# Feed-forward products in pairs of 64x128 tiles: a recurrent attention layer followed by a squared-ReLU feed-forward

## The chip, the cores and the metric

One NeuronCore of a Trainium2 chip runs the whole program. The metric is the device time of one execution in microseconds (us); lower is better. The engines are PE (TensorE: matrix products and transposes, with weight loads of their own), DVE (VectorE), ACT (ScalarE), POOL (GpSimd) and SP (SyncE, which here only issues DMAs).

## The reference

Four batches of eight heads, 768 steps, head dimension 40. Each head has a 40x40 state that is read, decayed and updated at every step; the outputs of all heads, put side by side, are the 320 features of 3072 tokens, which pass through a feed-forward of 320 to 2048 to 320 with a squared ReLU between.

```python
for t in range(S):                                # S = 768, state is B x H x D x D
    y[:, :, t] = einsum('bhd,bhde->bhe', rt, state)
    Sa = einsum('bhde,bhe->bhd', state, at)
    state_decay = state * wt[:, :, None, :] - einsum('bhd,bhe->bhde', Sa, bt)
    state = state_decay + einsum('bhd,bhe->bhde', vt, kt)
x = y.transpose(0, 2, 1, 3).reshape(B * S, H * D)  # 3072 x 320
h = x @ w_in                                       # 320 x 2048
g = maximum(h, 0) ** 2
out = g @ w_out                                    # 2048 x 320
```

## The kernel before

The steps are worked in 12 chunks of 64 steps, all 32 heads at once, so that a chunk gives 256 tokens. `load(c)` issues the six inputs of a chunk on SP, two DMAs each, into buffers that two chunks share in turn. `prep(c)` takes the logarithm of w on ACT, splits it in two bf16 parts (`hi`, `lo`), forms running sums and their exponentials on PE and ACT (`ci`, `cf`, `ei`, `ex`, `ef`), scales k and b (`mulKB`), casts a, r and v, and transposes them on PE (`TK`, `TA`, `TR`); `EN` is the first triangular product. `rec(c)` solves for the updates (`AS`, `EV`, `NU`) and carries the state on (`SC`, `S`, `TS`). `read(c)` has the outputs (`TV`, `CX`, `RS`, `Y`), multiplies them with the decay (`y`, and `yd` for 64 columns once more behind the 320), and transposes the 320 features of the 256 tokens (`XT`, copied by `xt`) into the tile `XT`, 3 x 256 columns on 128 partitions: two tiles of 128 features, and a third that holds the last 64 features on both partition halves.

`ffn(c)` is the feed-forward of the chunk's 256 tokens. The 2048 hidden units are four groups `u` of 512.

- `F c u`: 8 full products, weights of 128 features x 128 units from `WIN`, 256 columns.
- `FL c u`: the last 64 features, 4 products with weights of 64 x 128 from `WLAST`; the two halves of PE's rows take two products at a time (shape "R"). `FL` stands behind `F` for even `u` and before it for odd `u`.
- `f c u` applies the ReLU from PSUM into `G` (ACT or DVE), `q c u` squares it (DVE, POOL or ACT).
- `O c u`: 8 products with weights of 128 units x 128 tokens from `G` against 320 columns of `WOUT`; two halves `g` of the tokens lie in the two PSUM banks of one buffer. `o c` copies both halves, 128 x 640, to `osb`, `st c` stores them.

Every PE operation has a shape, the second argument of `pe`: "D" is the full 128 x 128 array, "R" two tiles of 64 rows, "C" two of 64 columns, "Q" 64 x 64 tiles. PSUM is used as four buffers `pb0` to `pb3` of two banks; the number behind PE in the order says which one an operation takes.

The program has no scheduler of its own. `ORDER` is a text of 1,030 or so entries, "engine operation", written out for all 12 chunks, and `Plan.issue` emits the operations in that order; each engine then runs its own operations in that order and waits by semaphore where data or buffers are not ready. The weights of the feed-forward are loaded in the first part of SP's queue (`lwl`, `lwi`, `lwo`) into the buffers of `G` and `osb`, and cast from there (`cwl`, `cwi`, `cwo`).

```python
ORDER = """SP ldw 0; SP lda 0; SP ldb 0; SP ldk 0; ACT ln 0; SP ldw 1; POOL hi 0; ...
... PE F 10 u3; ACT q 10 u1; PE0 F 11 u0; ACT f 10 u3; PE2 F 11 u2; ACT q 10 u0; DVE q 10 u3;
PE FL 11 u0; PE1 FL 11 u3; PE FL 11 u2; PE3 FL 11 u1; ACT f 11 u0; PE F 11 u1; ...
```

Of the kernel before, what the change touches and what calls it, by code (L numbers as in the profile page):

```python
# [84 lines left out]
HALVES = ()  # L85
O_AFTER = 0
ORDER = """SP ldw 0; SP lda 0; SP ldb 0; SP ldk 0; ACT ln 0; SP ldw 1; POOL hi 0; POOL castA 0; DVE lo 0; PE0
TA 0; SP lda 1; PE1 ci 0 h0; PE2 ci 0 h1; ACT ex 0 h0 g1; PE3 cf 0; ACT ex 0 h1 g0; ACT ei 0 h1;
ACT ex 0 h1 g1; ACT ei 0 h0; SP ldv 0; ACT ef 0; DVE mulKB 0 h1; SP ldw 2; ACT ex 0 h0 g0; DVE
mulKB 0 h0; DVE tA 0 g0; PE2 TK 0; DVE tK 0; ACT ln 1; SP ldk 1; POOL hi 1; DVE tA 0 g1; PE3 EN 0  # L90
g0; POOL lo 1; DVE mEN 0 g0; PE1 EN 0 g1; DVE mEN 0 g1; SP ldb 1; PE2 ci 1 h1; POOL castV 0 g0;
ACT ei 1 h1; POOL castV 0 g1; ACT ex 1 h1 g1; ACT ex 1 h1 g0; POOL castA 1; PE0 EV 0; SP ldr 1;
PE3 cf 1; ACT u0 0; PE1 ci 1 h0; ACT ln 2; PE NU 0; ACT ex 1 h0 g1; PE2 TA 1; POOL hi 2; ACT ef 1;
SP lda 2; DVE lo 2; ACT u1 0 g0; DVE tA 1 g0; ACT ei 1 h0; SP ldv 1; PE3 S 0 g0; DVE tA 1 g1; ACT
ex 1 h0 g0; ACT u1 0 g1; PE1 ci 2 h0; SP ldr 0; ACT ex 2 h0 g1; PE S 0 g1; DVE mulKB 1 h0; PE2 TV
0; DVE mulKB 1 h1; ACT ei 2 h0; DVE s 0 q1; ACT tV 0; SP ldw 3; PE0 TK 1; DVE s 0 q0; SP ldk 2;
DVE tK 1; PE3 TS 0; ACT tS 0; PE2 EN 1 g1; PE0 cf 2; DVE mEN 1 g1; SP ldb 2; PE3 EN 1 g0; ACT ef
2; POOL castR 0; DVE mEN 1 g0; ACT ex 2 h0 g0; POOL castV 1 g1; ACT castA 2; PE2 TR 0; PE0 ci 2
h1; POOL castV 1 g0; ACT tR 0 g0; PE1 AS 1; SP lwl 0; ACT tR 0 g1; POOL castR 1; PE EV 1; ACT ln
3; PE3 CX 0 g0; PE2 CX 0 g1; ACT u0 1; POOL hi 3; DVE mCX 0 g0; ACT ex 2 h1 g1; PE NU 1; POOL lo  # L100
3; ACT ex 2 h1 g0; SP lwi 0 u0; ACT ei 2 h1; DVE mCX 0 g1; PE3 TR 1; ACT u1 1 g0; PE0 TA 2; ACT tR
1 g1; DVE tA 2 g1; PE2 Y 0; SP ldv 2; ACT tR 1 g0; ACT u1 1 g1; PE3 SC 1; DVE mulKB 2 h1; PE1 TV
1; SP ldr 2; PE S 1 g0; DVE tA 2 g0; ACT tV 1; PE S 1 g1; DVE y 0; DVE mulKB 2 h0; ACT cwl 0; DVE
yd 0; PE0 TK 2; DVE s 1 q0; PE1 ci 3 h1; POOL cwi 0 u0; SP lwi 0 u1; PE2 CX 1 g0; DVE tK 2; ACT ei
3 h1; ACT ex 3 h1 g0; ACT ex 3 h1 g1; SP lwo 0 x1; DVE s 1 q1; PE0 cf 3; PE1 EN 2 g0; DVE mCX 1
g0; ACT ef 3; PE3 TS 1; POOL castV 2 g1; SP lwo 0 x0; ACT tS 1; DVE mEN 2 g0; PE0 EN 2 g1; POOL
castR 2; PE2 AS 2; SP ldb 3; POOL castV 2 g0; DVE mEN 2 g1; PE3 ci 3 h0; PE1 XT 0; ACT ex 3 h0 g0;
POOL cwi 0 u1; ACT ei 3 h0; DVE xt 0; PE EV 2; ACT ex 3 h0 g1; SP lwi 0 u3; PE0 CX 1 g1; ACT u0 2;
PE1 FL 0 u1; DVE mCX 1 g1; PE NU 2; SP lda 3; PE3 RS 1; ACT u1 2 g0; PE0 SC 2; PE Y 1; DVE u1 2
g1; SP ldk 3; PE F 0 u1; DVE y 1; SP lwi 0 u2; DVE yd 1; PE S 2 g0; ACT f 0 u1; PE S 2 g1; PE2 TR  # L110
2; DVE s 2 q0; PE3 FL 0 u3; ACT tR 2 g1; POOL cwi 0 u3; DVE s 2 q1; ACT tR 2 g0; SP ldw 4; DVE q 0
u1; POOL castA 3; PE F 0 u3; POOL cwo 0 x0; PE1 TV 2; ACT f 0 u3; DVE cwo 0 x1; PE2 XT 1; PE0 TS
2; SP lwo 0 x2; ACT tV 2; PE3 F 0 u0; DVE tS 2; POOL mulKB 3 h0; DVE xt 1; PE0 TA 3; PE FL 0 u0;
SP lwo 0 x3; DVE tA 3 g1; PE2 FL 1 u3; ACT f 0 u0; PE1 CX 2 g0; POOL cwi 0 u2; DVE tA 3 g0; PE F 1
u3; SP ldv 3; DVE mulKB 3 h1; PE3 F 1 u2; ACT f 1 u3; DVE mCX 2 g0; SP ldr 3; PE0 TK 3; ACT ln 4;
PE FL 1 u2; PE2 FL 1 u1; DVE tK 3; PE1 CX 2 g1; ACT f 1 u2; POOL hi 4; PE F 1 u1; POOL cwo 0 x2;
DVE mCX 2 g1; PE3 F 1 u0; POOL lo 4; ACT cwo 0 x3; PE0 EN 3 g0; ACT f 1 u1; SP lwo 0 x5; PE FL 1
u0; DVE mEN 3 g0; PE1 F 0 u2; ACT f 1 u0; SP lwo 0 x4; PE FL 0 u2; DVE q 0 u0; PE2 EN 3 g1; POOL
castV 3 g0; PE0 cf 4; ACT f 0 u2; DVE mEN 3 g1; PE3 ci 4 h0; SP ldw 5; POOL castV 3 g1; ACT ef 4;
PE1 RS 2; DVE q 0 u2; PE Y 2; ACT ei 4 h0; PE2 AS 3; DVE yd 2; PE EV 3; DVE cwo 0 x5; ACT ex 4 h0  # L120
g1; DVE y 2; PE0 O 0 u0; SP lwo 0 x7; ACT u0 3; POOL cwo 0 x4; DVE q 1 u0; ACT ex 4 h0 g0; POOL
castR 3; ACT q 0 u3; PE1 ci 4 h1; SP lwo 0 x6; PE NU 3; ACT ex 4 h1 g1; PE3 TR 3; ACT u1 3 g0; SP
ldk 4; PE O 0 u1; DVE tR 3 g1; ACT ex 4 h1 g0; DVE u1 3 g1; ACT ei 4 h1; PE O 0 u2; POOL cwo 0 x7;
SP ldb 4; ACT tR 3 g0; ACT ln 5; PE1 XT 2; DVE cwo 0 x6; PE2 TV 3; SP lda 4; POOL hi 5; DVE xt 2;
PE3 SC 3; ACT tV 3; PE S 3 g0; POOL lo 5; PE S 3 g1; PE O 0 u3; DVE s 3 q1; SP ldv 4; DVE s 3 q0;
POOL q 1 u1; PE1 ci 5 h0; ACT o 0; PE2 CX 3 g0; SP ldk 5; PE3 cf 5; ACT ex 5 h0 g0; DVE mCX 3 g0;
PE0 FL 2 u1; ACT ef 5; PE F 2 u1; DVE mulKB 4 h0; ACT ex 5 h0 g1; PE2 F 2 u2; ACT f 2 u1; SP ldb
5; DVE mulKB 4 h1; POOL castA 4; PE3 FL 2 u3; PE FL 2 u2; ACT ei 5 h0; DVE q 2 u1; PE0 TK 4; ACT f
2 u2; PE1 TA 4; PE F 2 u3; DVE tA 4 g0; SP ldw 6; DVE tK 4; PE2 F 2 u0; POOL castV 4 g0; ACT f 2
u3; POOL castV 4 g1; PE FL 2 u0; DVE tA 4 g1; PE0 ci 5 h1; POOL q 2 u3; ACT f 2 u0; PE3 CX 3 g1;  # L130
PE1 O 1 u0; SP lda 5; DVE mCX 3 g1; ACT ex 5 h1 g1; ACT q 2 u0; PE2 EN 4 g1; PE3 EN 4 g0; POOL q 1
u2; DVE mEN 4 g1; PE O 1 u1; ACT ex 5 h1 g0; ACT ei 5 h1; SP st 0; DVE mEN 4 g0; PE0 RS 3; PE Y 3;
POOL mulKB 5 h0; SP ldr 4; PE2 AS 4; DVE y 3; PE EV 4; DVE q 1 u3; PE O 1 u2; SP ldw 7; DVE yd 3;
ACT ln 6; DVE mulKB 5 h1; PE O 1 u3; ACT u0 4; POOL hi 6; POOL q 2 u2; PE NU 4; ACT o 1; PE3 XT 3;
ACT u1 4 g0; PE0 TS 3; SP st 1; DVE xt 3; PE1 TK 5; ACT tS 3; DVE u1 4 g1; PE3 FL 3 u3; POOL castA
5; PE F 3 u3; SP ldv 5; DVE tK 5; POOL castR 4; PE2 TA 5; ACT f 3 u3; POOL lo 6; PE0 TV 4; SP lda
6; DVE tA 5 g1; PE1 O 2 u0; DVE tA 5 g0; DVE tV 4; ACT ln 7; PE3 SC 4; PE S 4 g0; SP ldb 6; PE S 4
g1; PE2 ci 6 h0; DVE s 4 q0; PE0 TR 4; ACT ex 6 h0 g0; PE O 2 u1; SP ldk 6; ACT ei 6 h0; DVE s 4
q1; ACT ex 6 h0 g1; DVE tR 4 g1; ACT tR 4 g0; PE3 cf 6; PE2 EN 5 g0; ACT ef 6; POOL castV 5 g1; PE
O 2 u2; DVE mEN 5 g0; SP ldr 5; POOL castV 5 g0; ACT q 3 u3; PE0 CX 4 g0; PE3 ci 6 h1; DVE mCX 4  # L140
g0; PE2 CX 4 g1; ACT ei 6 h1; POOL hi 7; PE O 2 u3; ACT castA 6; POOL lo 7; DVE mCX 4 g1; PE0 F 3
u0; ACT ex 6 h1 g0; ACT o 2; ACT ex 6 h1 g1; PE FL 3 u0; SP st 2; PE2 EN 5 g1; PE1 TA 6; ACT f 3
u0; DVE mEN 5 g1; PE3 RS 4; PE Y 4; SP ldw 8; ACT q 3 u0; PE0 AS 5; POOL mulKB 6 h1; DVE yd 4; PE
EV 5; DVE tA 6 g1; PE2 FL 3 u1; DVE y 4; SP ldv 7; ACT u0 5; PE F 3 u1; POOL mulKB 6 h0; DVE tA 6
g0; PE3 F 3 u2; SP ldv 6; ACT f 3 u1; PE FL 3 u2; POOL castR 5; PE1 XT 4; PE2 TK 6; ACT f 3 u2;
DVE xt 4; POOL q 3 u1; PE NU 5; DVE tK 6; SP ldr 6; PE1 TR 5; ACT u1 5 g0; PE3 F 4 u0; DVE tR 5
g1; ACT tR 5 g0; ACT u1 5 g1; PE FL 4 u0; PE2 EN 6 g1; PE1 EN 6 g0; ACT f 4 u0; DVE mEN 6 g1; PE0
SC 5; SP lda 7; PE S 5 g0; PE S 5 g1; ACT q 3 u2; PE3 ci 7 h0; DVE s 5 q1; PE2 O 3 u0; SP ldk 7;
ACT ei 7 h0; DVE mEN 6 g0; ACT ex 7 h0 g1; PE O 3 u1; ACT ex 7 h0 g0; SP st0 0; DVE s 5 q0; POOL
castV 6 g0; PE3 TV 5; PE1 ci 7 h1; DVE tV 5; POOL castR 6; PE0 TS 4; ACT ex 7 h1 g1; SP ldb 7; PE  # L150
O 3 u2; ACT ei 7 h1; POOL castA 7; DVE tS 4; ACT ex 7 h1 g0; ACT ln 8; SP ldr 7; PE3 CX 5 g0; PE1
# [808 lines left out]
```

## Time and profile before

| | |
|---|---|
| median of 3 runs | 252.59 us (251.22, 252.59, 256.84) |
| span of the profiled execution | 249.1 us, mean granted PE clock 0.985 |
| device time of the profiled execution | not listed by itself; the runs lie 2.1, 3.5 and 7.7 us above its span |
| busy: PE, weight loads, DVE, ACT, POOL | 219.2, 171.4, 183.3, 172.4, 119.3 us |
| products on PE | 5752 |
| first and last group of products begin | 8.1 us, 239.4 us (`O 11 u0`) |
| `WOUT` products, 128 x 320 | 384, 57.2 us in all |
| `WIN` products, 128 x 256 | 384, 48.4 us |
| `WLAST` products, 64 x 256 | 192, 17.4 us |
| DMA | 33.58 MB, 135 GB/s over the span |

The span is the time from the first to the last instruction; the device time of a run has the start and the end around it. Busy time of PE is a union: products overlap in the pipeline, and the mean duration of one (some 0.27 us) is longer than the distance between two starts. A duration of a group is therefore no price of one product; the distance of starts is.

### The profile page before, as it was taken

The numbers are of one execution on the slowest core, as the hardware profiler recorded it, in microseconds if no ns is written. First come the engines' busy times: TensorE is split into PE (matmuls) and PEld (weight loads), VectorE is DVE, ScalarE is ACT, GpSimd is POOL, SyncE is SP. The second block draws the span as 40 slices with busy tenths as digits, with TensorE's granted clock in tenths as the row PEclk, the third lists the DMA queues.
The fourth block names the chain that finished last, engine by engine and source line by source line (L and its number), as shares of the span: only waits on it lengthen the run. The fifth ranks groups of instructions, "written<-read, shape, count | busy, mean of one in ns | idle before, by whom it ended". The sixth has DMA issues, their size and how long they took to land.

```text
span 249.1 us, 12580 instructions
## 1 busy us (share of the span) xinstructions
PE 219.2 (88%) x5752; PEld 171.4 (69%) x5752; DVE 183.3 (74%) x227; ACT 172.4 (69%) x231; POOL 119.3 (48%) x119
## 2 busy tenths in 40 slices
PE   0458868859997999999999999999999999999991
PEld 0336856647775777787778878877777787877770
DVE  7585869786976889976877958788778889746121
ACT  2548898737995876688759788896798351863930
POOL 4261332416746598383488881534369930452000
PEclk9999997799999999999999999999999999999999
DMA  6999899989998986978868978965580020201121
GB/s 130 168 157 212 158 190 182 229 195 218 224 195 161 157 199 122 189 159 147 184 171 136 179 121 217 157 163 115 119 144 4 4 58 4 56 3 30 26 52 55
DMA packets 115179, 33.58 MB, mean 135 GB/s; under 512 B 101302, under 2 KB 115126, under 8 KB 115126
## 3 DMA queue, kind: packets, MB, share of 16 engines
q1 hardware_dynamic: 114982, 32.62, 65.3%
q8 instruction: 45, 0.74, 1.2%
q10 hardware_dynamic: 144, 0.16, 0.2%
q14 instruction: 8, 0.07, 0.1%
HBM read 28.84 MB, written 3.93 MB: 132 GB/s over the span
## 4 chain that ended last, share of the span: by engine, by line
PE 51%; SPq 21%; DMA 8%; DVE 6%; ACT 6%; issue 4%; POOL 3%; POOLq 0%; ACTq 0%
PE pb L384 45%; SPq L407 8%; PE pb L388 5%; SPq L431 3%; SPq L421 3%; SPq L400 2%; SPq L882 2%; SPq L414 2%; DMA osb<-in_moe_w_out_dram 2%; DMA G<-in_moe_w_in_dram 2%; DMA raw_w<-in_w_dram 2%; DMA raw_r<-in_r_dram 2%; DVE AR L365 1%; ACT AR L370 1%; DMA out_dram<-osb 1%
## 5 line engine op out<-in xcount | busy, mean ns | idle before, releaser
L384 PE MATMUL pb<-WOUT,G 128*128 128x320 bf16 x384 | 57.2, 300 | 1.1 <-DVE WOUT L365 1.1
L802 ACT ACTIVATE G<-pb 128x1024 bf16<-128x1024 f32 x44 | 44.6, 1021 | 19.3 <-PE pb L384 18.4
L810 POOL TENSOR_TENSOR G<-G 128x1024 bf16<-128x1024 bf16 x21 | 40.8, 1956 | 24.2 <-ACT G L802 24.1
L384 PE MATMUL pb<-XT,WIN 128*128 128x256 bf16 x384 | 48.4, 273 | 2.8 <-POOL WIN L374 2.8
L384 PEld LDWEIGHTS <-G 128*128 128x128 bf16 x384 | 35.3, 98 | 15.8 <-issue 2.3
L384 PEld LDWEIGHTS <-WIN 128*128 128x128 bf16 x384 | 34.9, 98 | 10.4 <-POOL WIN L374 3.3
L578 DVE TENSOR_TENSOR CX<-pb,MSKI 128x1024 bf16<-128x1024 f32 x24 | 29.0, 1220 | 7.4 <-PE pb L384 7.3
L578 DVE TENSOR_TENSOR EN<-pb,MSK 128x1024 bf16<-128x1024 f32 x24 | 29.0, 1221 | 6.5 <-PE pb L384 6.2
L481 ACT ACTIVATE Gin<-pb 64x320 f32<-64x320 f32 x48 | 20.6, 429 | 9.8 <-PE pb L384 9.2
L374 POOL CAST VU<-raw_v 64x640 bf16<-64x640 f32 x24 | 18.7, 777 | 11.8 <-DMA raw_v<-in_v_dram 11.1
L370 ACT ACTIVATE osb<-pb 128x640 f32<-128x640 f32 (+1 forms) x13 | 8.3, 640 | 18.6 <-PE pb L384 18.1
L670 DVE TENSOR_TENSOR STb<-pb,GT 64x640 bf16<-64x640 f32 x22 | 18.0, 820 | 2.9 <-PE pb L384 2.6
L374 POOL CAST hi<-lnW 128x640 bf16<-128x640 f32 x12 | 9.0, 747 | 22.7 <-ACT lnW L453 19.4
L380 DVE TENSOR_TENSOR KB<-raw_kb,iG 128x640 bf16<-128x640 f32 x16 | 15.6, 992 | 5.7 <-DMA raw_kb<-in_b_dram 3.2
L384 PEld LDWEIGHTS <-EN 64*64 64x64 bf16 x768 | 15.3, 114 | 5.9 <-issue 2.7
L475 ACT ACTIVATE iG<-pb 128x640 f32<-128x640 f32 x24 | 16.7, 696 | 3.4 <-PE pb L384 3.2
L553 DVE TENSOR_TENSOR AR<-pb,GT 128x512 bf16<-128x512 bf16 x24 | 15.8, 683 | 2.3 <-PE pb L388 2.0
L384 PE MATMUL pb<-XT,WLAST 64*128 64x256 bf16 x192 | 17.4, 274 | 0.1
L808 DVE TENSOR_TENSOR G<-G 128x1024 bf16<-128x1024 bf16 x13 | 10.4, 805 | 8.6 <-ACT G L802 8.5
L370 ACT ACTIVATE VUT<-pb 128x2048 bf16<-128x2048 bf16 x8 | 15.0, 1874 | 2.2 <-PE pb L388 2.2
L370 ACT ACTIVATE VU<-pb 64x640 bf16<-64x640 f32 x19 | 13.2, 696 | 3.7 <-PE pb L384 3.5
L378 POOL TENSOR_TENSOR KB<-raw_kb,iG 128x640 bf16<-128x640 f32 x8 | 12.6, 1584 | 6.2 <-ACT iG L475 4.5
(82 smaller groups left out, 417.5 us busy)
## 6 DMA issues: line engine op xcount, KB each, us to landing
raw_w<-in_w_dram SPq DMA_DIRECT2D x24, 160.0 KB, 4.5
raw_a<-in_a_dram SPq DMA_DIRECT2D x24, 160.0 KB, 4.4
raw_kb<-in_b_dram SPq DMA_DIRECT2D x24, 160.0 KB, 4.3
...
```

What stands on the lines that cost most here:

```text
L370: alts.append(("ACT", c_act(n), lambda: nc.scalar.activation(out=o_(), in_=i_(), func=ACTF.Copy, scale=1.0 if scale is None else scale)))
L374: lambda: nc.gpsimd.tensor_copy(out=o_(), in_=i_())))
L380: ("DVE", c_dve(n), lambda: nc.vector.tensor_tensor(out=o_(), in0=a_(), in1=b_(), op=op))]
L384: return lambda: nc.tensor.matmul(out=o_(), lhsT=l_(), rhs=r_(), start=start, stop=stop, skip_group_check=True)
L407: nc.sync.dma_start(out=raw_kb[c % NKBR][rows(g if nm == "b" else 1 - g), NJ * g:NJ * g + NJ, :], in_=half(x, g))
L475: ew(f"ei {c} h{jh}", [("ACT", c_act(2 * n), lambda hb=hb, jh=jh: nc.scalar.activation(out=iG[0][:].rearrange("p (g j) e -> p g (j e)", g= ...
L481: nc.scalar.activation(out=Gin[c % NGI][rows(g), NP * jh:NP * jh + NP, :].rearrange("p j e -> p (j e)"), in_=slot(hb, FP32)[rows(g), g, 0: ...
L553: ew(f"tA {c} g{g}", [("DVE", c_dve(512), lambda g=g: nc.vector.tensor_tensor(out=steps(AR[q2][:, 0, g]), in0=turned(ha, g), in1=steps(GT[ ...
L578: evac(f"m{nm} {c} g{g}", lambda s, n: [("DVE", c_dve(n), lambda: nc.vector.tensor_tensor(out=dst[q2][:, g, s].rearrange("p q i t -> p (q ...
L670: ew(f"s {c} q{q}", [("DVE", c_dve(2 * n), lambda q=q: nc.vector.tensor_tensor(out=STb[q2][rows(q), :, q, 0:D], in0=slot(hs, FP32)[rows(q) ...
L802: ("ACT", c_act(1024), lambda gb=gb, hf=hf: nc.scalar.activation(out=gb, in_=slot(hf, FP32)[:], func=ACTF.Relu)),
L810: ("POOL", 1900, lambda gv=gv: nc.gpsimd.tensor_tensor(out=gv, in0=gv, in1=gv, op=ALU.mult)),
```

## The change

The tile `XT` becomes five tiles of 256 columns. Partitions 0 to 63 of tile k hold features 64k to 64k+63, partitions 64 to 127 the next 64, which for the last tile are the first 64 again (`yd` now copies columns 0 to 64). `XT` on PE has 20 transposes for 12, and `xt` copies 1280 columns for 768. `F` has 20 products with weights of 64 x 128, in ten pairs: the two partition halves work on two different blocks of units and two different tiles of features. `FL` is gone. `O` is split by `g`; for each, 32 products with 64 units each run in 16 pairs, one partition half into each PSUM bank of a buffer, so that the two banks have to be added: `oa` copies the first bank on ACT to `osb`, `o` adds the second on DVE. The last chunk's `O` keeps full products, in one bank for each `g`. The pieces of w_in are loaded by partition halves, 64 x 4 x 256 instead of 128 x 2 x 256. Constants and helpers that are not used any more are taken out (`evac` and `both` split nothing before). `ORDER` is written anew for all engines.

```diff
-    XT = buf("XT", [128, 3, NT], BF16, 2)
+    XT = buf("XT", [128, 5, NT], BF16, 2)
...
-    WIN = buf("WIN", [128, 2, DFF], BF16)[0]
+    WIN = buf("WIN", [128, 4, 4, 256], BF16)[0]
...
-        ew(f"yd {c}", out_y(n - 64, n, n), reads=[hy] + GIN, writes=[("Yb", q2, 1)],
+        ew(f"yd {c}", out_y(0, 64, n), reads=[hy] + GIN, writes=[("Yb", q2, 1)],
...
-        for k3 in range(3):
+        for k in range(5):
             for bb in range(2):
                 for g in range(2):
                     ms.append(tp(
...
-                        lambda k3=k3, bb=bb, g=g: Yb[q2][
-                            rows(g), bb, 128 * k3:128 * k3 + 128], g))
+                        lambda k=k, bb=bb, g=g: Yb[q2][
+                            rows(g), bb, 64 * k:64 * k + 128], g))
...
-            lambda: slot(hx, BF16)[:, :, 0:384].rearrange("p g (k t) -> p g k t", t=128),
-            768, True),
+            lambda: slot(hx, BF16)[:, :, 0:640].rearrange("p g (k t) -> p g k t", t=128),
+            1280, True),
...
-            for x in (1, 0) if tail else (0, 1):
-                if x:
-                    pe(f"FL {c} u{u}", "R", NT, ml, **last)
-                else:
-                    pe(f"F {c} u{u}", "D", NT, ms, **wide)
+            for i in range(2):
+                for k in range(5):
+                    for rg in range(2):
+                        f = (k + rg) % 5
+                        ms.append(mm(
+                            lambda rg=rg, i=i, hf=hf: slot(hf, FP32)[:, rg, NT * i:NT * i + NT],
+                            lambda rg=rg, f=f, i=i, u=u: (
+                                WLAST[rows(rg), u] if f == 4 else WIN[rows(rg), u, f])[
+                                :, 128 * i:128 * i + 128],
+                            lambda rg=rg, k=k: XT[q2][rows(rg), k, :],
+                            i == 0 and k == 0, k == 4))
+            pe(f"F {c} u{u}", "R", NT, ms, reads=[("XT", q2), ("WIN", u), ("WLAST",)],
+               writes=[hf], alloc=[hf])
...
+                    for h in range(2):
+                        ms.append(mm(
+                            lambda h=h, ho=ho: slot(ho, FP32)[:, h, 0:DM],
+                            lambda g=g, j=j, h=h: G[q2][
+                                rows(h), j, 2 * g * L:2 * g * L + 2 * L],
+                            lambda j=j, h=h: WOUT[rows(h), j, :], j == 0, j == NFB - 1))
+                pe(f"O {c} g{g}u{u}", "D" if final else "R", DM, ms,
+                   reads=[("G", q2, u), ("WOUT", 2 * u), ("WOUT", 2 * u + 1)],
+                   writes=[ho], alloc=[ho] if u == 0 else [])
+            if not final:
+                ew(f"oa {c} g{g}", copy_alts(
+                    lambda g=g: osb[q2][:, g, :],
+                    lambda ho=ho: slot(ho, FP32)[:, 0, 0:DM], DM, engines=("ACT",)),
+                   reads=[ho], writes=[("osb", q2, g)], free=[ho])
+                ew(f"o {c} g{g}", [("DVE", c_dve(DM), lambda g=g, ho=ho: nc.vector.tensor_tensor(
+                    out=osb[q2][:, g, :], in0=slot(ho, FP32)[:, 1, 0:DM],
+                    in1=osb[q2][:, g, :], op=ALU.add))],
+                   reads=[ho, ("osb", q2, g)], writes=[("osb", q2, g)], free=[ho])
+                continue
```

In the new order the end of the list reads:

```diff
+xt 11; ACT oa 10 g1; PE3 F 11 u2; DVE o 10 g1; ACT f 11 u2; PE0 F 11 u0; POOL q 11 u2; DVE f 11 u0;
+DVE q 11 u0; PE1 F 11 u1; ACT f 11 u1; PE3 F 11 u3; ACT q 11 u1; PE0 O 11 g1u0; SP st 9; DVE f 11
...
```

More of the change, by code (lines that the diff above doesn't have):

```diff
@@ L82, in issue @@
         assert len(done) == len(self.ops)
[L85 to L151, printed above, removed]
@@ new lines @@
+cwi 0 u3; ACT ef 4; SP ldv 3; PE0 ci 4 h0; DVE mulKB 3 h1; ACT ei 4 h0; ACT ex 4 h0 g1; SP ldr 3;
+PE1 F 1 u0; DVE tA 3 g0; DVE tA 3 g1; ACT ex 4 h0 g0; PE3 CX 2 g0; DVE mCX 2 g0; PE2 F 1 u1; PE3 TK
+3; ACT tK 3; DVE f 1 u1; POOL q 0 u1; PE0 RS 2; PE Y 2; POOL cwi 0 u2; POOL cwo 0 x3; DVE y 2; ACT
+f 1 u0; DVE yd 2; PE2 F 0 u3; DVE cwo 0 x2; PE3 EN 3 g1; PE0 F 1 u2; DVE f 0 u3; DVE mEN 3 g1; POOL
+castV 3 g1; ACT f 1 u2; PE1 F 0 u2; SP lwo 0 x5; PE2 EN 3 g0; DVE mEN 3 g0; ACT f 0 u2; PE0 F 1 u3;
@@ new lines @@
+1 u0; POOL cwo 0 x6; POOL mulKB 4 h1; DVE s 3 q1; ACT q 0 u3; DVE s 3 q0; PE0 F 2 u2; ACT f 2 u1;
+DVE hi 5; PE3 TV 3; ACT q 1 u1; PE O 0 g1u3; SP ldw 6; DVE lo 5; ACT f 2 u2; PE O 0 g0u3; SP ldv 4;
+ACT oa 0 g0; DVE tV 3; DVE q 1 u2; PE0 cf 5; POOL castA 4; DVE o 0 g0; PE3 F 2 u3; ACT oa 0 g1; DVE
+o 0 g1; ACT ef 5; POOL castV 4 g0; PE2 F 2 u0; DVE mulKB 4 h0; ACT f 2 u3; PE0 CX 3 g0; PE3 ci 5
+h0; SP ldk 5; ACT f 2 u0; ACT ei 5 h0; PE1 O 1 g0u0; SP ldb 5; DVE mCX 3 g0; PE O 1 g0u1; PE2 TK 4;
@@ new lines @@
+mulKB 5 h0; ACT u1 4 g1; ACT oa 1 g1; POOL mulKB 5 h1; DVE tS 3; PE3 TV 4; DVE o 1 g1; PE1 TK 5;
+PE0 SC 4; ACT f 3 u3; PE S 4 g0; DVE q 2 u3; SP ldv 5; ACT tV 4; DVE tK 5; PE S 4 g1; POOL castA 5;
+DVE s 4 q0; PE2 O 2 g0u0; PE1 ci 6 h0; PE O 2 g0u1; PE3 TA 5; DVE s 4 q1; ACT ex 6 h0 g1; PE O 2
+g0u2; POOL castR 4; PE O 2 g0u3; SP ldr 5; ACT ex 6 h0 g0; SP ldb 6; DVE tA 5 g0; ACT ei 6 h0; DVE
+tA 5 g1; PE1 EN 5 g0; PE0 TR 4; ACT oa 2 g0; DVE o 2 g0; POOL castV 5 g1; ACT tR 4 g1; PE3 O 2
+g1u0; DVE mEN 5 g0; ACT tR 4 g0; PE O 2 g1u1; PE2 CX 4 g1; PE0 cf 6; DVE mCX 4 g1; PE O 2 g1u2; PE1
@@ new lines @@
+ACT tK 9; DVE s 8 q1; PE0 ci 10 h0; DVE mCX 8 g1; PE O 6 g0u2; PE O 6 g0u3; PE3 O 6 g1u0; ACT ex 10
+h0 g1; PE1 EN 9 g1; PE O 6 g1u1; ACT oa 6 g0; DVE o 6 g0; ACT ex 10 h0 g0; PE2 CX 8 g0; POOL castV
+9 g1; ACT ei 10 h0; PE O 6 g1u2; DVE mEN 9 g1; PE0 cf 10; SP ldv 11; DVE mCX 8 g0; PE1 XT 7; PE O 6
+g1u3; PE2 TS 8; DVE xt 7; ACT ef 10; PE0 ci 10 h1; ACT oa 6 g1; DVE tS 8; DVE o 6 g1; PE1 F 7 u0;
+POOL mulKB 10 h0; ACT ex 10 h1 g1; PE2 EN 9 g0; ACT ei 10 h1; ACT ex 10 h1 g0; ACT f 7 u0; PE3 F 7
@@ L896, in weights @@
                     True, engines=("POOL", "ACT", "DVE")),
[L897 removed]
+                   reads=[("osb", x % 2, 0), ("osb", x % 2, 1)], writes=[("WOUT", x)])
     IDQ = buf("IDQ", [128, 128], BF16)[0]
```

310 lines of the change are left out of this document (155 added, 155 removed).

## The prediction

> **What bounds the kernel now.** First the busy tenths of the page and the chain, for where the end is set; then the timeline of the last stage, for what a product and a change of product shape cost; then the groups, for the price of what is added; last the busy times by stretch.
>
> ```profile
> PE   0458868859997999999999999999999999999991
> DVE  7585869786976889976877958788778889746121
> ACT  2548898737995876688759788896798351863930
> ...
> DMA  6999899989998986978868978965580020201121
> ...
> PE 51%; SPq 21%; DMA 8%; DVE 6%; ACT 6%; issue 4%; POOL 3%; POOLq 0%; ACTq 0%
> ```
>
> Up to slice 9 (56 us) PE has holes while DMA is at eight or nine tenths: the loads set the pace. From there PE is at nine tenths to the end, and the chain runs mostly through PE. So a change in PE's work after 56 us shows in the time, if PE stays the last to finish.
>
> ```profile
> 232.30 0.77 PEld L384 LDWEIGHTS <-WLAST 64*128 64x128 bf16 x16 [0.21 <-issue]
> 232.30 1.05 PE L384 MATMUL pb<-XT,WLAST 64*128 64x256 bf16 x16
> ...
> 233.28 0.77 PEld L384 LDWEIGHTS <-WIN 128*128 128x128 bf16 x8 [0.21 <-issue]
> 233.28 1.05 PE L384 MATMUL pb<-XT,WIN 128*128 128x256 bf16 x8
> ...
> 234.17 3.42 PE L384 MATMUL pb<-WOUT,G 128*128 128x320 bf16 x24
> ...
> 238.30 5.60 PE L384 MATMUL pb<-WOUT,G 128*128 128x320 bf16 x40
> ```
>
> The 16 half-height products run as 8 pairs: (1.05 - 0.27)/7 = 0.11 us a pair. The 8 full products: (1.05 - 0.27)/7 = 0.11 us each; the single starts in the trace are 109 ns apart in both. With 320 columns (5.60 - 0.30)/39 = 0.136 us. So a pair of half products costs what one full product costs. From 232.30 to 233.28 are 0.98 us, 8 x 0.11 is 0.88: the change from pairs to full tiles costs 0.10. From 233.28 to 234.17, full to full, are 0.89 us: nothing. Over the trace an unwaited change has a median of 96 ns (86 to 99 by kind).
>
> ```profile
> L740 DVE TENSOR_TENSOR Yb<-pb,Gin 128x640 bf16<-128x640 f32 x12 | 9.8, 817 | 1.0 <-PE pb L384 1.0
> L740 DVE TENSOR_TENSOR Yb<-pb,Gin 128x128 bf16<-128x128 f32 x12 | 3.4, 283 | 1.3 <-PE pb L384 1.3
> L365 DVE COPY XT<-pb 128x768 bf16<-128x768 bf16 x12 | 6.6, 553 | 3.4 <-PE pb L388 3.4
> L365 DVE COPY Sb<-pb 128x1280 bf16<-128x1280 bf16 x8 | 6.6, 820 | 2.4 <-PE pb L388 2.3
> L370 ACT ACTIVATE osb<-pb 128x640 f32<-128x640 f32 x11 | 7.7, 701 | 14.6 <-PE pb L384 14.5
> ```
>
> ```profile
> 75.00:100.00 25.00, 23.21 (x601) 17.63 (x601) 21.45 (x24) 17.47 (x22) 18.70 (x14) 1.00 0.80 160
> 100.00:125.00 25.00, 24.46 (x668) 19.11 (x662) 19.85 (x23) 19.79 (x29) 12.30 (x13) 1.00 0.86 170
> 125.00:150.00 25.00, 24.88 (x713) 19.59 (x713) 19.21 (x24) 19.89 (x26) 20.33 (x17) 1.00 0.80 149
> 150.00:175.00 25.00, 24.74 (x726) 19.46 (x717) 20.41 (x24) 19.85 (x24) 9.70 (x10) 1.00 0.75 166
> ```
>
> By stretch of 25 us, after the length: PE, weight loads, DVE, ACT, POOL. DVE and ACT are near 0.80: there is room, but not much.
>
> **The span as a sum.** Number of products in the written order times their spacing gives 184.8 us of PE work; the order has 181 changes of shape, 17.4 at 96 ns; together 202.1. A group's start less the work ahead of it is the delay gathered: 8.1 us at the first product, 34 at F 0 u0 (58.2 against 24.3), 41.6 at the last group. The end lies 5.4 behind: 202.1 + 41.6 + 5.4 = 249.1. Of the 7.6 gathered after F 0 u0, 5.3 are waits at the start of groups (1.2 of them O 0 u3 on w_out), the rest a few ns a product.
>
> **The change on PE.** F: 384 full products and 96 pairs become 480 pairs, 52.5 to 52.8 us. O: 352 full to 352 pairs, 0.136 either way (bounds: pairs of 320 columns in ci are 0.133 to 0.143 apart, so -0.9 to +2.5). XT: 4 more pairs of transposes a chunk at 0.029, 12 chunks, +1.4. Shape changes: 181 to 89 (one into the last chunk's O), -92 x 0.096 = -8.8. New sum 195.2, **-6.9 us**, all on the engine that sets the end.
>
> The Trainium skill ("TensorE: Matmul & The Clock Gate", Part 3, what overlaps) says that a weight load overlaps a running product only if the row group differs; the next pair's loads hit the rows of the running pair. By that rule each of the 832 pairs would add its 95 ns load, 79 us. The 16 loads and 16 products above lie in the same 1.05 us, so here the trace speaks against it.
>
> **The change beside PE.** Per chunk but the last, O's evacuation was one copy of 0.70 on ACT (11 in all). Now, for each g, ACT copies 320 and DVE adds 320 to it. ACT: between 0.30 (160 elements, last chunk) and 0.70 (640), 0.43 x 22 = 9.5, +1.8. DVE: between 0.283 (128) and 0.817 (640), 149 + 1.043 ns an element = 0.48, x 22 = +10.6 (6.2 and 18 with the ends, which is how far DVE's share below can move: 88% to 97%). xt takes 1280 elements: 0.82 (the row of Sb) for 0.55 on DVE. With the operations that the order gives to other engines (castV 7 times to ACT, mulKB 6 times to POOL, f on DVE 8 for 4) the totals by these rows are DVE 185.5 to 201.3, ACT 181.4 to 192.2, POOL 118.6 to 108.0. Back to back, DVE instructions overlap by 84 ns and ACT's by 105. With about that off each, the order's PE work from 41.8 (O 0 g1u2) to 167.0 (RS 10) has beside it 114.3 us of DVE, 91%, where before 100.4 lay beside 126.6, 79%; ACT 85% for 71%. In two stretches of some 20 us (PE work 41.8 to 62.1, 83.2 to 104.2) DVE is asked for 104% of PE's time.
>
> The new waits: the bank of an O half comes free only after ACT and then DVE; queued behind the add on DVE are tA, mEN, mCX, for which EN, EV and Y on PE wait. Of the hand-overs of a bank after PE work 41, those with under 0.5 us between the evacuation's least time and the next user's turn rise from 72 to 96.
>
> **Loads.** The first 39 entries of SP's queue are the same loads in another order, 72 us long. With each place's issue time of before, 4.2 us to land (4.3 in the page) and a cast, the new order needs a delay of 29 to 35 up to F of chunk 1 (34.3 before), and at most 38.2 later (ldb 8 at PE work 104.8; 37.8 before). Delays of 38 to 40 are there anyway, so the loads stay hidden, by a hair. Stores move back in the queue (st 1 from place 50 to 59); oa 3 needs it at about 118, it lands at about 118. The w_in pieces keep 256 rows of 1 KB. The cover costs 1 us for each us that the loads come later.
>
> **The sum.** Delay 34.0 at the loads, 2.3 small, 1.2 for w_out, the other 4.1 of waits x 96/72 = 5.5, and 0.9 for each 104% stretch = 1.7: 44.7. Span 195.2 + 44.7 + 5.4 = 245.3. The median 252.59 lies 3.5 above the span shown (fastest run 2.1, slowest 7.7), so **248.8 us**, 1.5% less. On its own 246 to 252.
>
> **Rivals.**
> *No new waits.* For it: PE waited only 5.3 us in 190 with DVE at 0.80, and copies have cover. Against: the 104%. Delay 41.6: 242.2 + 3.5 = 245.7.
> *DVE becomes the bound (slower).* For it: 114.3 us of DVE in 125.2 of PE, ACT 85% beside it, each O half through both in turn. If DVE stays at the mean 0.80 of 75 to 175 us, the stretch takes 114.3/0.80 = 142.9, +17.7: delay 34.0 + 17.7 + 1.2 = 52.9, span 253.5, time 257.0. Against: 0.86 was reached from 75 to 100, and DVE was not the bound then. It takes back the whole gain below a share of 0.83, and 2% more is lost below 0.79. The Trainium skill ("TensorEngine Tiling (Array Packing)", PSUM Bottleneck) warns of this: tiling helps TensorE, not the evacuation.
> *The loads come later.* The stores, or casts that now sit in ACT's queue, hold SP's queue back by 5 us: delay 43 at PE work 104.8, then 4 more: 247.6 + 3.5 = 251.
> *Weight loads not hidden in pairs*, as a mechanism of rows: the row of these loads has 95 ns, which 832 pairs (480 of F, 352 of O) would show in full: 248.8 + 79 = 328 us. Against: the 8 pairs at 0.11 us with their 16 loads inside.
>
> **How the numbers follow.** Forecast 0.45, no new waits 0.25, DVE 0.19, loads 0.10, weight loads 0.01. Two per cent, 247.5 and 257.6, is about what a measurement of this kernel tells from no change. Below 247.5 lie the second case and 0.12 of the forecast: 0.37. Above 257.6 lie most of the DVE case, whose 257.0 is its mildest form, and the weight loads: 0.19. Between: 0.44. The range goes from 244 to 258.
>
> **What would show it.** Right: changes of shape at 89, F and O pairs 0.110 and 0.136 apart, PE work 195; DVE's add near 0.48; delay near 34 at F 0 and 43 to 46 at the end, with waits of PE on DVE or ACT. Wrong: pair spacing above 0.12, a delay over 36 at F 0 (loads), DVE at nine tenths over several slices with PE at eight (DVE case), or waits no longer than 5 us (no new waits).

## The result, and the profile after

The changed kernel takes 266.15 us (median of four, 265.15 to 266.37) where the kernel before takes 253.19 beside it: a ratio of 1.051 (95%: 1.044 to 1.058). The forecast was 248.8 with a range of 244 to 258. The profiled execution has a span of 264.4 us. Ratios compare, for each kernel, only the executions within 1.5% of its fastest; a median in us is of all its executions.

From the page of the kernel after: busy time, busy tenths, one DMA queue, the chain by engine.

```profile
PE 219.1 (83%) x6584; PEld 184.1 (70%) x6584; DVE 200.7 (76%) x252; ACT 182.7 (69%) x253; POOL 108.3 (41%) x105
...
PE   0456798696998987889897978998979999999993
DVE  7557996689846995868877879898866958976671
...
q8 instruction: 51, 0.84, 1.3%
...
PE 62%; DVE 16%; ACT 9%; issue 8%; DMA 1%; SPq 1%; POOL 1%; DVEq 0%; ACTq 0%
```

PE no longer stands at nine tenths from slice 9 on. It has less to do and stands still more, and the chain has 8% "issue" for 4% before: time in which the engine waited for nothing that the profile shows. "Issue" also ends most of the idle time ahead of the products of F, and it stands high among the waits:

```profile
L367 PE MATMUL pb<-XT,WIN 64*128 64x256 bf16 x768 | 59.3, 269 | 3.6 <-issue 2.3
```

```profile
PEld L367 <- issue: 27.3, 47, 2.1
...
PE pb L367 <- issue: 11.4, 12, 1.9
```

The row of the weight loads (PEld) says little by itself, since before has one much like it:

```profile
PEld L384 <- issue: 22.6, 82, 1.1
```

The row of PE is the new one: in the waits of before there is no row in which PE waits for "issue" ahead of a product. Here are 12 such waits, up to 1.9 us each (the row of the transposes, L371, has 3 more). The longest in the timeline of PE and of its weight loads:

```profile
62.94 0.21 PE L367 MATMUL pb<-UTI,lo 64*128 64x64 bf16 x2
62.97 0.21 PE L367 MATMUL pb<-UTI,hi 64*128 64x64 bf16 x2
64.98 0.20 PE L367 MATMUL pb<-UTI,lo 64*128 64x64 bf16 x2 [1.80 <-issue]
...
64.98 0.10 PEld L367 LDWEIGHTS <-lo 64*128 64x128 bf16 x2 [1.92 <-issue]
```

This is the middle of `cf 4`: pairs 0.03 us apart, no semaphore to wait for, operands that have long been there, and then nothing for 2 us. What these places have in common is seen by counting. A product is two instructions, a weight load and a matmul. All 13 gaps of this kind after 45 us lie at instructions 178 to 190 of a run of 256, counted from the first product. The row of q8, the queue of kind "instruction", fits: 51 packets, and 2 x 6584 = 13168 instructions make 258 for each; before, 45 packets for 11504, 256 each.

```profile
q8 instruction: 45, 0.74, 1.2%
```

The trace has the time of each of these packets. Every one of the 13 gaps ends 1.3 to 1.8 us after a packet of q8 has ended; the gap above ends at 64.98, its packet at 63.68. The gaps of the same kind in the runs below end 1.1 to 1.8 us after one.

So PE's instructions come by DMA in blocks of 256, and PE waits when it has worked off a block before the next is there. Below, "border waits" of a run are the gaps of over 0.35 us, less 0.1, between two products that wait for no semaphore, after 45 us. Before: 0. After: **15.0 us**, of which 0.9 at 49.8 us, ahead of F 0. (The expectations below have 15.7, a count that took in gaps from 0.25 us.)

The rows that answer to those shown of before, from the groups with shapes kept apart, and the busy times by stretch (length, PE, weight loads, DVE, ACT, POOL):

```profile
L812 DVE TENSOR_TENSOR osb<-pb,osb 128x320 f32<-128x320 f32 x22 | 10.6, 485 | 3.8 <-ACT osb L353 3.7
L353 ACT ACTIVATE osb<-pb 128x320 f32<-128x320 f32 x22 | 9.3, 434 | 12.7 <-PE pb L367 11.9 <-DMA raw_w<-in_w_dram 0.6
```

```profile
75.00:100.00 25.00, 22.35 (x624) 17.85 (x618) 17.97 (x23) 21.51 (x31) 10.34 (x9) 1.00 0.87 180
100.00:125.00 25.00, 21.90 (x760) 19.44 (x758) 18.80 (x25) 18.55 (x27) 9.84 (x10) 1.00 0.83 171
125.00:150.00 25.00, 21.22 (x694) 17.81 (x692) 19.87 (x22) 18.50 (x25) 18.08 (x16) 1.00 0.71 136
150.00:175.00 25.00, 21.80 (x679) 18.85 (x674) 21.79 (x26) 19.04 (x29) 8.09 (x7) 1.00 0.70 135
```

The new DVE and ACT instructions have the forecast size. PE is busy 87% of these 100 us where it was busy 97%, and no other engine is at its limit instead (DVE 78%, ACT 78%). Nor is it the clock: in both profiled executions it was 0.5 for 6.8 us, all ahead of F 0, and full from there until the last products were done.

The sum of the prediction, measured, in us:

| | before | forecast | after |
|---|---|---|---|
| PE work with changes of shape | 202.1 | 195.2 | 195.2 |
| delay at F 0 u0 | 34.0 | 34.0 | 37.3 |
| border waits after it | 0 | 0 | 14.1 |
| other delay after it | 7.6 | 10.7 | 13.3 |
| behind the last group | 5.4 | 5.4 | 4.5 |
| span | 249.1 | 245.3 | 264.4 |

### The profile page after: what moved, and what is told of

The parts are those of the page before. It is cut to its first block, busy times and chain, and to the rows that moved or that the text cites. A ratio compares the mean times of both kernels' runs of the same rounds, so it can differ in the third digit from the quotient of the medians.

```text
span 264.4 us, 14288 instructions
## 1 busy us (share of the span) xinstructions
PE 219.1 (83%) x6584; PEld 184.1 (70%) x6584; DVE 200.7 (76%) x252; ACT 182.7 (69%) x253; POOL 108.3 (41%) x105
## 4 chain that ended last, share of the span: by engine, by line
PE 62%; DVE 16%; ACT 9%; issue 8%; DMA 1%; SPq 1%; POOL 1%; DVEq 0%; ACTq 0%
PE pb L367 54%; PE pb L371 9%; DVE CX L561 2%; DVE EN L561 2%; ACT Gin L464 2%; ACT iG L458 2%; DVE STb L653 2%; DVE G L777 2%; DMA raw_kb<-in_k_dram 1%; DVE AR L536 1%; DVE AR L348 1%; DVE KBT L348 1%; DVE G L773 1%; ACT AR L353 1%; ACT GT L480 1%
## 5 line engine op out<-in xcount | busy, mean ns | idle before, releaser
L367 PE MATMUL pb<-WOUT,G 64*128 64x320 bf16 (+1 forms) x736 | 62.3, 297 | 2.0 <-issue 0.8
L367 PE MATMUL pb<-XT,WIN 64*128 64x256 bf16 x768 | 59.3, 269 | 3.6 <-issue 2.3
L367 PEld LDWEIGHTS <-WIN 64*128 64x128 bf16 x768 | 44.9, 94 | 7.5 <-issue 3.7
L367 PEld LDWEIGHTS <-G 64*128 64x128 bf16 (+1 forms) x736 | 36.1, 94 | 13.0 <-DVE G L777 1.3
L367 PE MATMUL pb<-XT,WLAST 64*128 64x256 bf16 x192 | 35.3, 269 | 0.6 <-issue 0.6
L367 PEld LDWEIGHTS <-WLAST 64*128 64x128 bf16 x192 | 17.8, 94 | 1.5 <-issue 0.8
L536 DVE TENSOR_TENSOR AR<-pb,GT 128x512 bf16<-128x512 bf16 x24 | 15.8, 682 | 2.8 <-ACT GT L480 1.6
L781 ACT ACTIVATE G<-G 128x1024 bf16<-128x1024 bf16 x17 | 17.8, 1053 | 0.1
L361 POOL TENSOR_TENSOR lo<-lnW,hi 128x640 bf16<-128x640 f32 x10 | 14.0, 1399 | 7.0 <-ACT hi L353 4.9
L723 DVE TENSOR_TENSOR Yb<-pb,Gin 128x640 bf16<-128x640 f32 (+1 forms) x24 | 12.6, 552 | 4.3 <-PE pb L367 4.3
L353 ACT ACTIVATE KBT<-pb 128x2048 bf16<-128x2048 bf16 x6 | 11.3, 1877 | 6.1 <-PE pb L371 6.1
```

The costliest lines, as they stand in the source:

```text
L353: alts.append(("ACT", c_act(n), lambda: nc.scalar.activation(out=o_(), in_=i_(), func=ACTF.Copy, scale=1.0 if scale is None else scale)))
L361: return [("POOL", 40 + 2.35 * n, lambda: nc.gpsimd.tensor_tensor(out=o_(), in0=a_(), in1=b_(), op=op)), ("DVE", c_dve(n), lambda: nc.vect ...
L367: return lambda: nc.tensor.matmul(out=o_(), lhsT=l_(), rhs=r_(), start=start, stop=stop, skip_group_check=True)
L536: ew(f"tA {c} g{g}", [("DVE", c_dve(512), lambda g=g: nc.vector.tensor_tensor(out=steps(AR[q2][:, 0, g]), in0=turned(ha, g), in1=steps(GT[ ...
L781: ("ACT", c_act(1024), lambda gv=gv: nc.scalar.activation(out=gv, in_=gv, func=ACTF.Square))],
```

## The experiments

Theory A: the border waits are waits for instructions, and come from their number and the speed at which they are worked off. Theory B: the new hand-over of O's banks with the add on DVE. Theory C: the new order of loads and casts. Ratios are to the kernel before on the same chip; "after" and "before" name the kernel that was edited. The edits are shown shortened to the lines that matter.

| run | PE instructions | border waits, us | ratio (95%) |
|---|---|---|---|
| before | 11504 | 0 | 1 |
| after | 13168 | 15.0 | 1.051 (1.044 to 1.058) |
| e1: before, F and O split in halves | 13040 | 8.9 | 1.031 (1.021 to 1.040) |
| e2: after, add of 16 columns | 13168 | 17.5 | 1.054 (1.047 to 1.062) |
| e3: after, half of the transposes | 11920 | 5.5 | 1.016 (1.008 to 1.023) |
| e4: after, O in full products | 12464 | 11.0 | 1.071 (1.064 to 1.077) |
| e5: before, F in pairs | 12464 | 7.4 | 1.025 (1.020 to 1.031) |
| e6: new order, products of before | 11504 | 4.0 | 1.056 (1.042 to 1.070) |
| e7: after, no input loads from chunk 4 | 13168 | 4.9 | 1.014 (1.002 to 1.025) |
| e8: before, half of the transposes | 10256 | 1.2 | 0.990 (0.983 to 0.997) |
| e10: e5 and e8 together | 11216 | 1.2 | 1.008 (1.003 to 1.012) |
| e14: before, no input loads from chunk 4 | 11504 | 0.5 | 0.989 (0.978 to 1.000) |
| e15: e5 and e14 together | 12464 | 1.6 | 1.007 (1.003 to 1.012) |
| e12: e5, w_in by 128 partitions | 12464 | 8.0 | 1.025 (1.018 to 1.032) |
| e19: e15, w_in by 128 partitions | 12464 | 1.0 | 0.991 (0.987 to 0.996) |
| e18: after, w_in by 128 partitions | 13168 | 14.6 | 1.047 (1.037 to 1.057) |
| e20: e3 and e7 together | 11920 | 0 | 1.011 (1.005 to 1.016) |

### More instructions for the same work in the kernel before

```diff
-    ms.append(mm(out[:, 0:256], WIN.., XT[:, k2, :]))
+    for z in (0, 128):
+        ms.append(mm(out[:, z:z + 128], WIN.., XT[:, k2, z:z + 128]))
```

(and O's 320 columns as two times 160)

> The kernel before, with every full product of F and of O issued as two products of half the columns (128 or 160): the same result, 1536 PE instructions more (13040 instead of 11504, near the 13168 of the changed kernel), PE work longer by some 2 us, all else as it was. Theory A (PE's instruction fetch: a block of 256 instructions can't be worked off in less than some 4.5 us while loads run): waits of PE at a fixed place of every block of 256 instructions, inside groups that wait for nothing, 8 to 16 us in all, time 260 to 268. Theory B (DVE and the hand-over of banks through ACT and DVE) and theory C (the new order of loads and casts) see nothing new here: 255, no such waits.

```profile
PE pb L384 <- issue: 6.3, 11, 1.4
...
PE pb L388 <- issue: 1.2, 2, 0.9
```

Order, loads, banks and columns are those of before; 1536 instructions are added, and, by the spacing of the halves (0.056 and 0.069 us), some 2 us of PE work. The waits of the kernel after appear, 8.9 us at the same place of the blocks, and the time grows by 3.1%, some 8 us.

### Fewer instructions for the same work in both kernels

```diff
-            for x in range(2):
+            for x in range(1 if c >= 2 else 2):      # transposes, one of each pair
```

The copies behind them keep their size. A transpose alone takes PE as long as the pair.

> The changed kernel, from chunk 2 on with only the first of the two transposes of each pair in TK, TV, TS, TA and TR; the copies read the first bank twice, so the copies' work and the order are as they were and part of the result is left out. PE's work is the same, since a pair takes the time of one, but 1248 PE instructions are gone (11920 instead of 13168). Theory A: the waits at the block borders fall from 15.7 us to under 6, time 253 to 259. Theories B and C: 264 to 267, as ACT, DVE, POOL and the loads have the same work in the same order.

> The kernel before with only the first of each pair of transposes in TK, TV, TS, TA and TR from chunk 2 on (copies read the first bank twice; part of the result is left out): 10256 PE instructions for 11504, the same PE work and order. Theory A: before has no border waits, so there is nothing to win, 0 to 1 us faster than before. If fewer PE instructions were faster in themselves, or the transposes' second halves cost PE time of their own, 5 to 10 us faster; then the run with half of the transposes in the changed kernel shows less than it seems to.

The same edit takes 3.3% off the kernel after (1.051 to 1.016), as theory A expected, and 1% (2.5 us) off the kernel before, where it expected at most 1 us. That 1% is not firm: over all executions the medians lie 0.2% apart (255.2 and 255.8 us). So up to 1% of the gain of e3 may have another cause than the border waits. Of 15.0 us of these in the kernel after, 5.5 are left.

### The add on VectorE

```diff
-    out=osb[q2][:, g, :], in0=slot(ho, FP32)[:, 1, 0:DM],
+    out=osb[q2][:, g, 0:16], in0=slot(ho, FP32)[:, 1, 0:16],
```

> The changed kernel, with DVE's add of the second bank of O cut to 16 of 320 columns, so that most of the second half of the sum is left out; some 22 x 0.3 us less on DVE, and each bank is free 0.3 us sooner. Theory A: 263 to 266, the waits at the block borders stay. Theory B: a good part of the 13 us comes back, 252 to 258. Theory C: 264 to 266.

DVE's busy time falls from 200.7 to 194.9 us, the time does not (1.054), and 17.5 us of border waits are there. So the length of the add is not the cause. The hand-over itself, ACT first and then DVE, is still in this run and is not tried alone.

### The fetch by itself

The streams run twice, first without and then with the input loads:

```diff
+    for cols in (192, 160, 128, 96, 64):
+        for _ in range(64 * 6):
+            for h in range(2):
+                nc.tensor.matmul(out=t[:, h, 0:cols], lhsT=UTI[rows(h), :], rhs=mov[rows(h), 0:cols], ...)
```

> Nothing of the kernel is computed. TensorE runs 64x128 pairs only, 64 pairs (256 instructions) to a block, six blocks each at 192, 160, 128, 96 and 64 columns; first with no load on the queues, then the same again while SyncE sends all the input loads of the twelve chunks. From the spacing of pairs in the traces (110 ns at 256 columns, 29 ns at 64, linear between) a block would take 5.3, 4.5, 3.6, 2.7 and 1.9 us. Theory A (blocks of 256 instructions are fetched, and a block worked off faster than the next one arrives is waited for): with no loads the block time stops falling at some floor of 2 to 3.5 us, so that the 64-column blocks, and perhaps those of 96, take longer than 1.9 and 2.7; with loads the floor lies at 4 to 4.7 us and the 128-column blocks wait too; the waits stand at one place of each block. Rival (the waits in the kernel come from the products, banks or other engines): 1.9 us blocks in both stretches and no wait at any place.

Groups with shapes kept apart (busy, mean ns, idle before and its cause), both stretches together:

```profile
L915 PE MATMUL pb<-mov,UTI 64*128 64x160 bf16 x1536 | 53.5, 229 | 0.0
L915 PE MATMUL pb<-mov,UTI 64*128 64x128 bf16 x1536 | 44.3, 216 | 4.8 <-issue 4.8
L915 PE MATMUL pb<-mov,UTI 64*128 64x96 bf16 x1536 | 35.4, 203 | 12.9 <-issue 12.8
L915 PE MATMUL pb<-mov,UTI 64*128 64x64 bf16 x1536 | 27.1, 196 | 19.4 <-issue 19.3
```

From the starts in the trace, us for a block of 256 instructions (128 products):

| columns | 64 x pair spacing | without loads | with loads (DMA busy 0.85) |
|---|---|---|---|
| 192 | 5.3 | 5.28 | 5.28 |
| 160 | 4.4 | 4.43 | 4.43 |
| 128 | 3.6 | 3.57 | 4.28 to 4.83 |
| 96 | 2.7 | 2.99 to 3.73 | 3.79 to 5.31 |
| 64 | 1.9 | 3.24 to 4.00 | 3.35 to 5.17 |

(In the row of 64 columns with loads the granted clock was 0.5 from 243.4 to 246.8 us and from 263.9 us on, so its two ends are less sure.) Every wait stands in front of the 96th product of its block. So where PE would be faster than the fetch, a block mostly takes 3.5 to 3.7 us, and mostly 4.3 to 4.8, at times 5.3, with the input loads running: a floor a little above the one that theory A had said. The rival is out. Before asks for 256 instructions every 202.1/44.9 = 4.5 us of work, which lies within the floor under loads; after asks every 195.2/51.4 = 3.8, below it and barely above the floor without loads.

### The fetch and the loads

```diff
-                for g in range(2):
+                for g in range(2 if c < 4 else 0):     # every input's DMAs
```

> The changed kernel without the loads of r, k, v, w, a and b from chunk 4 on (those chunks work on the data of chunks 2 and 3), so that DMA is nearly quiet after some 80 us; instructions on PE, DVE, ACT and POOL as they are. Theory A with the fetch held up by the loads: blocks of 256 instructions come down from 4.3 to 4.5 us towards the 3.1 to 3.7 of the last stage, border waits after 90 us under 2 us, time 248 to 256. Theory A with a fetch that takes its time whatever the loads do: border waits stay, 262 to 266. Theory B: 263 to 267. Theory C: 252 to 260, with no border waits changed and PE's other waits gone.

> The kernel before without the loads of the inputs from chunk 4 on (older data are used again). Work on TensorE and instructions as before (202.1 us, 11504). If loads set part of the pace after F 0, the delay that grew from 36.9 us at chunk 4 to 41.1 us at the end falls by 2 to 4 us: 249 to 252 us where the kernel before runs at 253 to 255. If only TensorE sets the pace there: no change. No waits at block borders in either case.

Without the loads the border waits of the kernel after fall from 15.0 to 4.9 with all its instructions, as the floor of the run before this says. The kernel before gains 1%, at the edge of its interval (0.978 to 1.000), and has one border wait of 0.5 us where none was expected. The 259.1 us of e7 are above the 248 to 256 that were expected, which the next run explains in part.

### Both reliefs together

> The kernel after with both: half of the transposes left out from chunk 2 (1248 instructions fewer, the same work) and no input loads from chunk 4. Each alone cut the border waits to about 5 us and the time by 7 us. Theory A: together under 1.5 us of border waits are left and the delay at the end is 64.7 - 15 = 49 to 51 us, 1 to 2 less as loads wait for nothing: a span of 247 to 250, a median of 249 to 253, which is what the forecast without the fetch came to. If other waits take their place: 255 to 259.

After 45 us no border wait is left (one of 1.35 us stands at 42.0), but the ratio is 1.011 (255.6 us). That is no longer the 249 to 253 of theory A but the case in which other waits take their place. The profiled execution, with a span of 256.2 us, is the longest of the twelve (257.87 us). PE's longest waits after 45 us:

```profile
PE pb L367 <- DVE AR L547: 2.8, 3, 1.2
PE pb L367 <- ACT KBT L353: 1.1, 1, 1.1
PE pb L371 <- DVE KB L363: 1.0, 1, 1.0
```

Added up by engine, PE waits there 7.6 us for DVE and 4.0 for ACT; in the kernel after 5.7 and 2.6 beside 13.6 of issue; before 1.8 and 1.1. With 15.0 us of border waits gone the delay is 56.1 where it was 64.7, 8.6 less: 3.3 more are waited for DVE and ACT, and 3.2 are lost already at `cf 4` (41.5 for 38.3). Most of the latter is the clock's: 2.4 of it arise between 57.5 and 63.8 us, where the products of F 0 run at half pace. The granted clock from 50 to 64 us is 0.51 in this execution, 0.76 in that of the kernel after. DVE is at 0.86 of the time from 75 to 175 us in this run, PE at 0.94.

### O back to full products

Each half has one bank again, and ACT and DVE copy half of its columns each:

```diff
-                    if final:
+                    if True:      # O: full 128-row products in one bank
...
-                ew(f"o {c} g{g}", [("DVE", ..., nc.vector.tensor_tensor(... op=ALU.add))],
+                ew(f"o {c} g{g}", [("DVE", ..., nc.vector.tensor_copy(...[:, DM // 2:DM]))],
```

> The kernel after, with the O products as full 128-row products as before (one bank per half, no add on VectorE left to do for them beyond the copy), F kept in pairs. Work on TensorE by the spacings 203.5 us (+8.3), 177 shape changes, 12464 instructions in place of 13168. Theory A: waits at block borders fall from 15.7 us to 6 to 9 us, about what the kernel before with F in pairs and the same 12464 instructions showed (7.4), so the time stays within 265 to 269 us although the work grows by 8. Theory C and any other in which the waits do not hang on the number of instructions: 272 to 276 us.

The span is 268.1: 3.7 more than the kernel after for 8.3 more work. Border waits fell by 4.0, the whole delay by 4.6. The direction is that of theory A, but the waits fell by less than expected (11.0 are left), so the time missed the expectation by 2 us.

### The order alone

The products, tiles and loads of w_in of before in the new order (O's halves `g` still one after the other, each copied half by ACT and half by DVE, without an add):

> The new order with the products of before: each F group as 2 pairs and 8 full products, XT with 12 transposes, O full in one bank per g with two half copies, no add. 264 changes of shape instead of 89, PE work by the spacings of before 210.1 us, 11504 PE instructions as in before. Theory A: nearly no waits at block borders (under 3 us), although the order is the new one, and the loss of 15 us of shape changes against the changed kernel is about met by that: 260 to 266. Theory C (the order itself costs the time): waits of PE as long as in the changed kernel on top of 210, 270 to 278. Theory B: 258 to 264, without add and hand-over.

1.056, or 270.4 us: above the 260 to 266 of theory A and at the low end of the 270 to 278 of theory C. In this order the old products change shape 264 times (210.1 us of work for 202.1). With the 11504 instructions of before there are 4.0 us of border waits where A expected under 3. What the profiled span has beyond work grows from 47.0 to 54.7, by 3.7 more than these waits. So theory C is right in part: the order has a price of its own. It is dear for the old products, and the new ones take 15 us of work off it; of that 0.5% arrives, within the intervals.

### F in pairs in the order of before

F and FL as 16 and 4 products in pairs, with the tiles, `xt` and w_in loads of after; everything else, the order too, as before.

> The part of the change that concerns the first product alone, in the order of before: F and FL as pairs of 64x128 tiles with x on both partition halves, O as before. Shape changes fall from 181 to 134, PE work from 202.1 to 199.5, PE instructions rise from 11504 to 12464. Theory A: waits at block borders of 4 to 10 us eat the gain, 253 to 259. Theories B and C (neither the split of O nor the new order is in it): 250, the gain of 2.6 us comes through.

> F as pairs in the order of before, and again half of the transposes left out from chunk 2 on: 11216 PE instructions, 134 changes of shape. Theory A: with the instructions back under the number of before, border waits are under 2 us and the gain of the 47 changes of shape shows, 2 to 3.5 us faster than before with half of the transposes. Theory B or C, or a price of pairs that I have not seen: no faster than before with half of the transposes, or slower.

> The kernel before with F in pairs (12464 instructions), again without input loads from chunk 4 on; to be compared with the same without pairs. With loads the pairs cost 2.5% (6 us). If that is the fetch of instructions slowed by loads, late loads at chunk 8 and 3 to 4 us of late w_in at the first two chunks of F, then without the loads only the last stays beside 2 to 3 us of border waits (7.4 with loads) and 3.1 us less work: 2 to 4 us slower than without pairs. If the pairs themselves are slow in this order, the difference stays at 6 us or more.

With 3.1 us less work e5 is 2.5% slower (261.2 us, above the 253 to 259 of theory A). And e10 is 1.7% slower than e8 where both have only 1.2 us of border waits, which theory A does not give: that expectation failed. Without the input loads (e15 against e14) it is 1.8%. How large this rest is stays unsure, since the medians of all executions lie 0.8% (257.3 and 255.2 us) and 0.2% (254.5 and 253.9) apart. The trace of e15 shows one long wait, at `F 0 u3`, on PE and on POOL:

```profile
52.83 0.38 PE L384 MATMUL pb<-XT,WLAST 64*128 64x256 bf16 x4
58.61 1.25 PE L384 MATMUL pb<-XT,WIN 64*128 64x256 bf16 x10 [5.40 <-POOL WIN L374]
```

```profile
57.52 1.04 POOL L374 CAST WIN<-G 128x1024 bf16<-128x1024 f32 x1 [8.29 <-DMA G<-in_moe_w_in_dram]
```

In e14 this cast begins at 53.20. The pieces of w_in now go by 64 partitions a DMA: SP's issue of one takes 0.60 us at least (`after`), that of 128 partitions 0.37 (e8; 0.42 in `before`), and the queue is full there. Whether that is the cause was tried by sending them as before, which puts the weights in the wrong places:

```diff
-    out=stage(i)[rows(rg)].rearrange("p (k x) -> p k x", k=4), in_=wi[u, rg]
+    out=stage(i).rearrange("p (k x) -> p k x", k=2)[:, :, 256 * h:256 * h + 256], in_=wi[u][:, :, ...]
```

> The kernel before with F in pairs, but w_in sent to the staging buffer by the two DMAs of the kernel before (128 partitions each) in place of two of 64 partitions each: the weights then lie in the wrong places, the work and its instructions are the same (199.5 us, 12464). With 64-partition DMAs the pairs cost 2.5% (6 us). If the late w_in is a part of it (PE waited 2.3 to 5.7 us for WIN at the first F in three runs with pairs, where it waited 0.2 to 3.1 us without): 3 to 5 us of the 6 go, ratio to before 1.005 to 1.015, the rest being border waits of 7 us less 3.1 us of work. If the layout of the loads does not matter: 1.02 to 1.03 as before.

> The same without the loads of the inputs from chunk 4 on. Border waits about 1.6 us as in the run of the pairs without those loads. If late w_in was what made that run 4.6 us slower than the kernel before without those loads, this one comes to 249 to 252 us, ratio 0.98 to 0.995. If the pairs cost by something else, it stays at 1.005 or more.

> The kernel after with w_in sent by DMAs of 128 partitions (weights in the wrong places, work and instructions unchanged). The delay at the first F was 37.3 us where 34.0 was forecast. If the 64-partition loads of w_in are a part of these 3.3 us, 1 to 3 us go: 263 to 265 us, ratio 1.04 to 1.047. If the new order hides them: no change, 1.05.

Without later loads it is worth 1.6% by the ratios (e15 1.007, e19 0.991, intervals apart), but the medians of all twelve executions are 254.5 and 254.1 us, so its size is unsure. With the loads it is worth nothing (e5 and e12 1.025): the delay is 2.0 us smaller at `EN 3` (67 us) and 0.6 larger at `XT 2` (80 us). Between the two the granted clock of e12 was 0.5 for 3.4 us, from 76.6 us on, where that of e5 was full, so part of this loss is the clock's. In the kernel after it changes nothing that the intervals tell (1.047, 1.051). So late w_in is likely a part of what F in pairs costs in the order of before, and no run shows that it made the kernel after late. Where e19's 3.1 us less work go against e14 stays open.

## Why the prediction was wrong

- **The change on PE**: the failed step. Its terms hold: 89 changes of shape, pairs of F 0.110 and of O 0.136 us apart, PE work 195.2. It priced products by spacing and left out that the same work now takes 13168 instructions for 11504, and that they have to arrive. That term was put at nothing. Measured: 15.0 us of border waits, of the 19.1 by which the span was missed. The row of q8 with 45 packets stood in the page of before; 11504/45 = 256 was there to be read, the price of a late block was not.
- **Loads**, 34.0 at F 0: too low by 3.3. The sign given for that was late loads, but 0.9 of it is the border wait at 49.8 us, and PE waits up to 58 us for DVE 6.5 us in place of 2.5, and 7.2 with the old products in the new order (e6). So the rest is likely the order. F 0 begins at 58.3 as before (58.2), with 3.3 us less work done.
- **The change beside PE**: the add takes 0.485 us (forecast 0.48), the copy on ACT 0.434 (0.43), DVE in all rises by 17.4 us to 200.7 (forecast +15.8), POOL falls by 11.0 to 108.3 (-10.6), ACT rises by 10.3 to 182.7 (+10.8). The 192.2 of the forecast for ACT is a sum of rows, which already for before lay 9 us above the page (181.4 for 172.4). Waits on DVE and ACT after 45 us are 8.3 us; the two terms for them were 5.5 and 1.7, about right, and all delay but the border waits after F 0 came to 13.3 for 10.7.
- **No new waits**: excluded by the border waits.
- **DVE becomes the bound**: DVE's share from 75 to 175 us is 0.78, under the 0.79 from which this case was to lose 2%, but PE's waits for it are small and e2 gains nothing from a cheaper add. A low share showed that another thing held PE up. DVE comes to the fore only when the border waits are gone (e20).
- **The loads come later**: loads matter, but by slowing the fetch (e7).
- **Weight loads not hidden**: excluded by the spacing of 0.110 us.

By the table, the 19.1 us by which the span was missed are 15.0 of border waits, 2.4 of other delay ahead of F 0 and 2.6 behind it, less 0.9 at the end. Taking the fetch's part away gives back less than 15.0, since other waits follow: by e20 it is about 10 of the 17 us between 248.8 and 266.15 (1.051 to 1.011). The two edits of e20 are worth up to 1% each in the kernel before, which has no border waits, so it may be 5 to 10. For the other delay e6 points to the new order; no run splits it further.
